# Moving part of a fused attention and mixer kernel's transposes from TensorE to the DMA crossbar

## The chip, the cores and the metric

The kernel runs on one core of a Trainium2 chip. The metric is device microseconds (us) of one execution, the median of several runs. Before the change it is 288.36 us (three runs, 288.26 to 288.44). Beside the times there is one profiled execution, whose span from the first to the last instruction is 287.1 us.

## The reference

Block-sparse attention over 4 batches with 8 heads, 768 positions and 64 elements for each head, and then a token mixer and a channel mixer on its result:

```python
# attention: q, k, v are [4, 8, 768, 64]; the mask is made of 32x32 blocks
scores = scale * np.matmul(q, k.transpose(0, 1, 3, 2))
mask = np.abs(blk_i - blk_j) <= window          # window = 1, and the edge blocks,
...                                             # and 3 sampled blocks for each row of blocks
scores = np.where(mask, scores, -1000000000.0)
attn = np.exp(scores - max) / sum
x = (attn @ v), heads side by side               # [4, 768, 512]

# mixer
h = np.maximum(xt @ w_tok1, 0.0) @ w_tok2        # xt is x transposed: mixes the 768 tokens
u = x + h.transpose(0, 2, 1)
h2 = np.maximum(u @ w_ch1, 0.0) @ w_ch2          # mixes the 512 channels, 1536 in the middle
return u + h2                                    # float32
```

## The kernel before

Two heads form a pair; there are 16 pairs, four in each batch. The work is put in order by a small planner inside the kernel's Python code: it keeps an expected time for each engine, holds streams of TensorE work by priority (scores first, then attention times V, then transposes, then the token mixer, then the channel mixer), and emits whatever is ready first. The chip then executes each engine's instructions in exactly that order, and waits where an operand is not there.

One pair's Q and K come in by DMA, are put by VectorE into a layout with the two heads side by side, are transposed by TensorE in six blocks of 128x128, and are copied out of PSUM, one head at a time, into `ktb` and `qtb`. Rows 64 to 87 of these hold the block mask, so that the scores' matmul over 88 rows adds it:

```python
def transposes(p):
    ...
    lays = relayout(p)                          # VectorE: kraw -> klay, qraw -> qlay, vraw -> vaug
    for nm, bufs, there in (("k", ktb, kT_there), ("q", qtb, qT_there)):
        for c in range(NC):                     # NC = 6
            nc.tensor.matmul(out=box["t"][:, c, :], lhsT=lays[nm][:, c, :, :]...,
                             rhs=ident[:, :], ..., is_transpose=True)
            deps = [lays[nm + "ev"]]
            if p >= NV:                         # NV = 4 sets of ktb and qtb
                deps.append(qk_done[p - NV])
        for hd in range(2):                     # copies out of PSUM, by VectorE or ScalarE
            nc.vector.tensor_copy(out=buf[0:64, :], in_=i)          # L439
...
# scores, exponentials (L470, L478): 12 steps for each pair, 192 in all
nc.tensor.matmul(out=ps[:, hd, 0:384], lhsT=ktb[n][0:88, 128*j : 128*j+128],
                 rhs=qtb[n][0:88, 384*half : 384*half+384])         # twice in a step
nc.scalar.activation(out=et[:, :, :], in_=ps[:, :, 0:384], func=AF.Exp, scale=0.125)
# attention times V (L520): 6 small matmuls in a step
nc.tensor.matmul(out=po[:, hd, c, :], lhsT=et[:, hd, 128*c : 128*c+128], rhs=va[:, hd, j, 0:65])
```

The token mixer of a batch (L578, L603) leaves `u`, in two halves `g` of 256 channels. `u` is transposed by TensorE (L628), six blocks for each of four groups of 128 channels, and copied out of PSUM (L641), since the channel mixer needs the channels on the partitions:

```python
for dmc in (2 * g, 2 * g + 1):
    for sc in range(NC):
        nc.tensor.matmul(out=tbox["pt"][:, sc, :], lhsT=st[b]["u"][:, sc, 128*dmc : 128*dmc+128],
                         rhs=ident[:, :], ..., is_transpose=True)   # L628
    evac ...                                                        # L641
# channel mixer: 96 matmuls of 384 columns (L664) and 72 of 512 (L686) for each batch
nc.tensor.matmul(out=pbox["pm"][:, 0:384], lhsT=w_ch1[:, dmc, 128*cc : 128*cc+128],
                 rhs=st[b]["uT"][:, dmc, 384*sh : 384*sh+384], ...)
nc.tensor.matmul(out=pbox["pm"][:, :], lhsT=box["rc"][:, cc, 128*sc : 128*sc+128],
                 rhs=w_ch2[:, cc, :], ...)
```

Transposes and both mixers share three PSUM buffers (`psM`, tag `pm`). While an exponential is pending, the planner gives ScalarE nothing else.

Of the kernel before, what the change touches and what calls it, by code (L numbers as in the profile page):

```python
# [50 lines left out]
class Planner:  # L51
# [11 lines left out]
    def __init__(self, slots):  # L63
        self.now = 0.0
        self.free_at = {"pe": 0.0, "act": 0.0, "dve": 0.0}
        self.streams = []
        self.ops = []
        self.count = 0
        self.slots = {tag: [Ev(0.0)] * n for tag, n in slots.items()}
        self.exp_pending = 0  # L70
# [6 lines left out]
    def op(self, engines, cost, deps, emit, prio=5, lat=60.0):  # L77
        done = Ev()
        self.ops.append((prio, self.count, engines, cost, deps, emit, done, lat))
        self.count += 1  # L80
        return done
# [21 lines left out]
    def step(self):  # L103

        nxt = []
        moved = False
        if self.free_at["pe"] <= self.now:
            for s in self.streams:
                while s[3] is None or (callable(s[3]) and s[3]()):
                    s[3] = next(s[2], False)  # L110
                if s[3] is False or callable(s[3]):
                    continue
                cost, deps, tags, emit, done = s[3]
                t = self.when(deps, tags)
                if t is None:
                    continue
                if t <= self.now:
                    s[3] = None
                    emit()
                    if self.trace is not None:  # L120
                        self.trace.append((self.now, "pe", s[0], cost))
                    self.free_at["pe"] = self.now + cost
                    if done is not None:
                        done.t = self.now + cost + self.PE_LAT + self.SEM
                    moved = True
                    break
                nxt.append(t)
            self.streams = [s for s in self.streams if s[3] is not False]
        else:
            nxt.append(self.free_at["pe"])  # L130
        for eng in ("act", "dve"):
            if self.free_at[eng] > self.now:
                nxt.append(self.free_at[eng])
                continue
            best = None
            for o in self.ops:
                prio, num, engines, cost, deps, emit, done, lat = o
                if eng not in engines:
                    continue
                if eng == "act" and prio > 0 and self.exp_pending:  # L140
                    continue
                t = self.when(deps)
                if t is None:
                    continue
                if t <= self.now:
                    if best is None or (prio, num) < best[:2]:
                        best = o
                else:
                    nxt.append(t)
            if best is not None:  # L150
                prio, num, engines, cost, deps, emit, done, lat = best
                self.ops.remove(best)
                emit(eng)
                c = cost[eng]
                if self.trace is not None:
                    self.trace.append((self.now, eng, prio, c))
                self.free_at[eng] = self.now + c
                done.t = self.now + c + lat + self.SEM
                moved = True
        if moved:  # L160
            return True
        later = [t for t in nxt if t > self.now]
        if not later:
            return False
        self.now = min(later)
        return True
# [3 lines left out]
def kernel(  # L170
# [22 lines left out]
    NET = 8  # L193

# [14 lines left out]
    qtb = [sb1.tile([128, S], BF16, name=f"qtb{n}") for n in range(2 * NV)]  # L209
    ktb = [sb1.tile([128, S], BF16, name=f"ktb{n}") for n in range(2 * NV)]  # L210

    P = Planner({"ps": 2, "po": 1, "pm": 3, "et": NET, "a_t": 2, "o": 3, "rc": 2,
                 "lay": 2, "kq": NV, "va": NV})
# [112 lines left out]
    rows_there = {("k", n): Ev() for n in range(2 * NV)} | {("q", n): Ev() for n in range(2 * NV)}  # L326

    def mask_stream():
# [15 lines left out]
        for h in range(2):  # L344
            def copy(eng, h=h):
                nc.scalar.copy(out=qtb[0][R, 384 * h : 384 * h + 384], in_=pms[h][R, 0:384])
            e2.append(P.op(("act",), {"act": 420.0}, [done], copy, prio=0))
            rels[h].same_as = e2[h]
        rows_there["q", 0].same_as = e2[1]
        for n in range(2 * NV):  # L350
            for nm, bufs in (("k", ktb), ("q", qtb)):
                if (nm, n) == ("q", 0):
                    continue

                def copy(eng, n=n, nm=nm, bufs=bufs):
                    nc.vector.tensor_copy(
                        out=bufs[n][R, :], in_=indf if nm == "k" else qtb[0][R, :]
                    )
                rows_there[nm, n].same_as = P.op(
                    ("dve",), {"dve": 300.0}, e2, copy, prio=2 if n < 2 else 6  # L360
                )
# [5 lines left out]
    ones_there = [Ev() for _ in range(NV)]  # L367

# [14 lines left out]
    def relayout(p):  # L383
        lays = {}
        for nm in ("k", "q", "v"):
# [3 lines left out]
            def emit(eng, nm=nm, raw=raw):  # L389
                if nm == "v":  # L390
                    nc.vector.tensor_copy(out=vaug[p % NV][:, :, :, 0:64], in_=raw[:, :, :, :])  # L391
                    return
                lay = sbw.tile([128, NC, 2, D], BF16, tag=f"{nm}lay", bufs=2, name=f"{nm}lay{p}")
                nc.vector.tensor_copy(  # L394
                    out=lay[:, :, :, :], in_=raw[:, :, :, :].rearrange("p h c d -> p c h d")
                )
                lays[nm] = lay
# [4 lines left out]
            if nm != "v" and p >= 2:  # L402
                deps.append(qT_there[p - 2, 1])
# [4 lines left out]

    def transposes(p):
        for hd in range(2):  # L410
            kT_there[p, hd], qT_there[p, hd] = Ev(), Ev()
        yield lambda: ("v", p) in raws
        lays = relayout(p)
        for nm, bufs, there in (("k", ktb, kT_there), ("q", qtb, qT_there)):
# [15 lines left out]
            n_left = [2]  # L430
            for hd in range(2):
                buf = bufs[2 * (p % NV) + hd]

                def evac(eng, hd=hd, buf=buf, box=box):
                    i = box["t"][64 * hd : 64 * hd + 64, :, :].rearrange("p c s -> p (c s)")
                    if eng == "act":
                        nc.scalar.copy(out=buf[0:64, :], in_=i)
                    else:
                        nc.vector.tensor_copy(out=buf[0:64, :], in_=i)  # L439
# [17 lines left out]
    def qk_stream():  # L457
        for s in steps:
# [4 lines left out]
            def emit(s=s, done=done, rel=rel):  # L463
# [4 lines left out]
                for hd in range(2):  # L468
                    n = 2 * (p % NV) + hd
                    nc.tensor.matmul(  # L470
                        out=ps[:, hd, 0:384], lhsT=ktb[n][0:88, 128 * j : 128 * j + 128],
                        rhs=qtb[n][0:88, 384 * half : 384 * half + 384], start=True, stop=True,
# [3 lines left out]
                def exp(eng):  # L476
# [13 lines left out]
                [e for hd in range(2) for e in (  # L490
                    kT_there[p, hd], qT_there[p, hd],
                    rows_there["k", 2 * (p % NV) + hd], rows_there["q", 2 * (p % NV) + hd],
# [8 lines left out]
    def pv_stream():  # L501
        for s in steps:
# [3 lines left out]
            def emit(s=s, done=done):  # L506
# [23 lines left out]
                def norm(eng):  # L530
                    if b not in xs:
                        xs[b] = sbw.tile([128, NC, DM], BF16, tag="x", bufs=B, name=f"x{b}")
# [3 lines left out]
                        out=free(xs[b][:, 3 * half, 128 * pb : 128 * pb + 128], 0,  # L536
                                 [[64, 2], [DM, 3], [1, 64]]),
# [29 lines left out]

    def tok(b, g):
# [3 lines left out]
        for t in range(2):  # L572
            for sc in range(NC):
                def emit(t=t, sc=sc):
                    if t == 0 and sc == 0:
# [4 lines left out]
                        rhs=xs[b][:, sc, 256 * g : 256 * g + 256],  # L580
# [4 lines left out]
        if b not in st:  # L585
            st[b] = dict(u=xs[b], uT_there=[Ev() for _ in range(4)])
# [6 lines left out]
        for s2 in range(3):  # L593
# [16 lines left out]
            def add(eng, s2=s2, ubox=ubox):  # L610
                nc.vector.tensor_tensor(  # L611
                    out=st[b]["u"][:, 2 * s2 : 2 * s2 + 2, 256 * g : 256 * g + 256],
                    in0=ubox["pm"][:, :, :],
                    in1=xs[b][:, 2 * s2 : 2 * s2 + 2, 256 * g : 256 * g + 256], op=ALU.add,
# [5 lines left out]
        alias(a_rel, last)  # L620
        for dmc in (2 * g, 2 * g + 1):
            last, rel, tbox = Ev(), Ev(), {}
            for sc in range(NC):
                def emit(sc=sc, dmc=dmc, rel=rel, tbox=tbox):
                    if sc == 0:
                        P.take("pm", rel)
                        tbox["pt"] = psM.tile([128, NC, 128], BF16, tag="pm", name=f"pm_ut_{b}_{dmc}")
                    nc.tensor.matmul(  # L628
                        out=tbox["pt"][:, sc, :], lhsT=st[b]["u"][:, sc, 128 * dmc : 128 * dmc + 128],
                        rhs=ident[:, :], start=(sc == 0), stop=(sc == NC - 1), is_transpose=True,  # L630
                    )
                yield 56.0, [u_evs[sc // 2]], [("pm", 1)] if sc == 0 else [], emit, last if sc == NC - 1 else None

            def evac(eng, dmc=dmc, tbox=tbox):
                if "uT" not in st[b]:
                    st[b]["uT"] = sbw.tile([128, 4, S], BF16, tag="uT", bufs=B, name=f"uT{b}")
                o, i = st[b]["uT"][:, dmc, :], tbox["pt"][:, :, :].rearrange("p c s -> p (c s)")
# [9 lines left out]
    def ch(b, pool, tag):  # L647
# [4 lines left out]
        for cc in range(12):  # L652
            for sh in range(2):
                last, rel, pbox = Ev(), Ev(), {}
                for dmc in range(4):
                    first = dmc == 0
                    def emit(cc=cc, sh=sh, dmc=dmc, rel=rel, pbox=pbox):
                        if dmc == 0:
# [7 lines left out]
                            rhs=st[b]["uT"][:, dmc, 384 * sh : 384 * sh + 384],  # L666
# [11 lines left out]
                rc_there[cc, sh] = ev  # L678
        for sc in range(NC):
# [12 lines left out]
            def fin(eng, sc=sc, pbox=pbox):  # L692
                o = sbw.tile([128, DM], FP32, tag="o", bufs=3, name=f"o{b}_{sc}")
                nc.vector.tensor_tensor(  # L694
                    out=o[:, :], in0=pbox["pm"][:, :], in1=st[b]["u"][:, sc, :], op=ALU.add
# [37 lines left out]
    P.stream(-1, mask_stream())  # L733
    tok2_op = P.op(("dve",), {"dve": 900.0}, [tok2_raw], wtok2_lay, prio=3)
# [57 lines left out]
```

The softmax here doesn't subtract the row's maximum and nothing guards it: scores larger than these inputs give would overflow.

## Time and profile before

| | before |
|---|---|
| time, median of 3 | 288.36 us |
| span of the profiled execution | 287.1 us |
| ScalarE, exponentials (L478) | 192 instructions, 143.2 us busy |
| TensorE, transposes of K and Q (L421) | 96 + 96 instructions |
| TensorE, transposes of u (L628) | 96 instructions |
| VectorE, copies of transposed K and Q (L439) | 59 instructions, 552 ns each (5 more on ScalarE) |
| VectorE, copies of transposed u (L641) | 15 instructions, 553 ns each (1 more on ScalarE) |
| TensorE, channel mixer, first product (L664) | 384 instructions |
| last load of K, Q or V issued | 91.5 us |

In the profile each engine has a row of busy time and of instructions. PE is TensorE's matmuls and PEld its weight loads, DVE is VectorE, ACT is ScalarE, POOL is GpSimd and SP is SyncE. Matmuls overlap in the pipeline and a matmul's listed duration is from its start to its modelled end, so the time that one matmul costs TensorE is read from the distance between the starts of neighbours, and not from its duration.

### The profile page before, as it was taken

Reading aid. Unit: us, or ns where it says so; the run is one execution under the profiler, and the core shown is the slowest. Engines: PE = TensorE matmul, PEld = TensorE weight load, DVE = VectorE, ACT = ScalarE, POOL = GpSimd, SP = SyncE. Lnnn points to the kernel's source line nnn. Section 1 sums busy time; section 2 is a strip of 40 time slices with the busy share of each in tenths; the row PEclk is TensorE's granted clock in tenths of the full one; section 3 lists DMA queues with packets and bytes.
Section 4 is the critical chain, followed back from the end, with each engine's and each line's share of the span. In section 5 each row is a group of like instructions: output and inputs, shape, how many; then the busy total and the mean of one; then the engine's idle time right before and its main releaser. Section 6 shows DMA issues by size and latency. Waiting matters only on the chain.

```text
span 287.1 us, 6351 instructions
## 1 busy us (share of the span) xinstructions
PE 269.9 (94%) x2682; PEld 175.5 (61%) x2690; DVE 130.2 (45%) x286; ACT 191.9 (67%) x286; POOL 45.0 (16%) x70
## 2 busy tenths in 40 slices
PE   0799899999999999999999999999999999999994
PEld 0366676678777777777777754456544654456441
DVE  5789966557777569765546341210022001200121
ACT  1589999999999999999999642037501770067200
POOL 7956554522211000000000000000000000000000
PEclk9999999999999999999999999999999999999999
DMA  4999999996254100000000001220022001210122
GB/s 55 134 204 202 214 201 205 201 185 87 39 73 66 23 2 2 0 2 3 2 0 2 2 0 39 106 76 0 2 110 84 29 0 73 94 54 0 38 102 82
DMA packets 19168, 20.07 MB, mean 70 GB/s; under 512 B 1348, under 2 KB 15428, under 8 KB 19140
## 3 DMA queue, kind: packets, MB, share of 16 engines
q0 software_dynamic: 15648, 13.37, 30.3%
q1 hardware_dynamic: 3492, 6.29, 5.8%
q8 instruction: 21, 0.34, 0.5%
q14 instruction: 7, 0.06, 0.1%
HBM read 26.74 MB, written 6.29 MB: 115 GB/s over the span
## 4 chain that ended last, share of the span: by engine, by line
PE 73%; ACT 14%; DVE 6%; issue 2%; DMA 2%; POOL 2%; POOLq 0%; DVEq 0%; ACTq 0%
PE pm_ch L686 22%; PE pm_ch L664 21%; ACT et L478 14%; PE ps L470 14%; PE po L520 8%; PE pm_tok L578 3%; PE pm_tok L603 2%; DMA kraw<-in_k_dram 2%; DVE qtb L439 1%; PE pm_ut L628 1%; PE tq L421 1%; DVE ktb L439 1%; PE tk L421 1%; DVE x L535 1%; DVE klay L394 1%
## 5 line engine op out<-in xcount | busy, mean ns | idle before, releaser
L478 ACT ACTIVATE et<-ps 128x768 bf16<-128x768 f32 x192 | 143.2, 810 | 4.2 <-PE ps L470 3.2
L470 PE MATMUL ps<-qtb,ktb 88*128 88x384 bf16 x384 | 95.3, 329 | 4.0 <-ACT et L478 1.7
L560 ACT ACTIVATE rc<-pm_ch 128x384 bf16<-128x384 f32 x84 | 41.2, 491 | 60.7 <-PE pm_ch L664 44.8
L520 PEld LDWEIGHTS <-et 128*128 128x128 bf16 x1152 | 56.0, 97 | 22.8 <-DVE x L535 1.9
L664 PE MATMUL pm_ch<-uT,w_ch 128*128 128x384 bf16 x384 | 68.6, 326 | 0.2 <-DVE rc L562 0.2
L686 PE MATMUL pm_ch<-w_ch,rc 128*128 128x512 bf16 x280 | 62.4, 379 | 0.4
L520 PE MATMUL po<-vaug,et 128*128 128x65 bf16 x1152 | 61.5, 193 | 0.5 <-ACT et L478 0.2
L694 DVE TENSOR_TENSOR o<-pm_ch,x 128x512 f32<-128x512 f32 x24 | 16.6, 692 | 98.7 <-PE pm_ch L686 98.7
L664 PEld LDWEIGHTS <-w_ch 128*128 128x128 bf16 x384 | 37.0, 98 | 23.1 <-issue 0.3
L686 PEld LDWEIGHTS <-rc 128*128 128x128 bf16 x288 | 28.2, 98 | 33.6
L470 PEld LDWEIGHTS <-ktb 88*128 88x128 bf16 x384 | 34.2, 99 | 11.9 <-issue 4.4
L439 DVE COPY ktb<-tk 64x768 bf16<-64x768 bf16 x29 | 16.0, 552 | 17.5 <-PE tk L421 17.2
L611 DVE TENSOR_TENSOR x<-pm_tok,x 128x512 bf16<-128x512 f32 x24 | 16.2, 687 | 6.8 <-PE pm_tok L603 6.5
L535 DVE TENSOR_TENSOR x<-po,recip 128x384 bf16<-128x384 f32 x32 | 17.8, 557 | 1.1
L439 DVE COPY qtb<-tq 64x768 bf16<-64x768 bf16 x30 | 16.6, 552 | 2.1 <-PE tq L421 1.1
L603 PE MATMUL pm_tok<-a_t,w_tok 128*128 128x256 bf16 x96 | 17.0, 272 | 0.0
L230 POOL DMA_DIRECT2D vraw<-in_v_dram x16 | 12.3, 766 | 28.4 <-DVE vaug L391 25.7
L578 PE MATMUL pm_tok<-x,w_tok 128*128 128x256 bf16 x96 | 16.3, 272 | 0.0
L230 POOL DMA_DIRECT2D kraw<-in_k_dram x16 | 11.6, 727 | 7.7 <-DVE recip L534 2.2
L230 POOL DMA_DIRECT2D qraw<-in_q_dram x16 | 11.5, 720 | 6.4 <-DMA w_ch<-in_moe_w_ch_dram 2.4
L534 DVE RECIPROCAL recip<-po 128x6 f32<-128x6 f32 x32 | 6.2, 195 | 12.0 <-PE po L520 11.6
L421 PE MATMUL tq<-ident,qlay 128*128 128x128 bf16 x96 | 11.3, 230 | 0.2 <-DVE qlay L394 0.2
(49 smaller groups left out, 122.8 us busy)
## 6 DMA issues: line engine op xcount, KB each, us to landing
out_dram<-o SPq DMA_DIRECT2D x24, 256.0 KB, 2.0
kraw<-in_k_dram POOLq DMA_DIRECT2D x16, 192.0 KB, 7.9
qraw<-in_q_dram POOLq DMA_DIRECT2D x16, 192.0 KB, 7.4
vraw<-in_v_dram POOLq DMA_DIRECT2D x16, 192.0 KB, 7.0
w_ch<-in_moe_w_ch_dram POOLq DMA_DIRECT2D x8, 384.0 KB, 9.8
w_tok<-in_moe_w_tok_dram POOLq DMA_DIRECT2D x1, 384.0 KB, 7.8
w_tok2r<-in_moe_w_tok_dram POOLq DMA_DIRECT2D x1, 384.0 KB, 9.0
samp<-in_sampled_blocks_dram SPq DMA_DIRECT2D x1, 0.6 KB
```

The lines of the kernel that those rows point to most:

```text
L230: nc.gpsimd.dma_start(out=raw[:, :, :, :], in_=APx(src, 2 * p * S * D, [[NC * D, 128], [S * D, 2], [1, NC * D]]),)
L421: nc.tensor.matmul(out=box["t"][:, c, :], lhsT=lays[nm][:, c, :, :].rearrange("p h d -> p (h d)"), rhs=ident[:, :], start=(c == 0), stop=( ...
L439: nc.vector.tensor_copy(out=buf[0:64, :], in_=i)
L470: nc.tensor.matmul(out=ps[:, hd, 0:384], lhsT=ktb[n][0:88, 128 * j : 128 * j + 128], rhs=qtb[n][0:88, 384 * half : 384 * half + 384], star ...
L478: nc.scalar.activation(out=et[:, :, :], in_=ps[:, :, 0:384], func=AF.Exp, scale=0.125)
L520: nc.tensor.matmul(out=po[:, hd, c, :], lhsT=et[:, hd, 128 * c : 128 * c + 128], rhs=va[:, hd, j, 0:65], start=(j == 0 and hd == 0 and c = ...
L535: nc.vector.tensor_tensor(out=free(xs[b][:, 3 * half, 128 * pb : 128 * pb + 128], 0, [[64, 2], [DM, 3], [1, 64]]), in0=po[:, :, :, 0:64], ...
L560: nc.scalar.activation(out=o(), in_=i, func=AF.Relu)
L578: nc.tensor.matmul(out=box["pm"][:, t, :], lhsT=w_tok1[:, sc, 128 * t : 128 * t + 128], rhs=xs[b][:, sc, 256 * g : 256 * g + 256], start=( ...
L603: nc.tensor.matmul(out=ubox["pm"][:, i, :], lhsT=w_tok2[:, t, 2 * s2 + i, :], rhs=a_t[:, t, :], start=(i == 0 and t == 0), stop=(i == 1 an ...
L664: nc.tensor.matmul(out=pbox["pm"][:, 0:384], lhsT=w_ch1[:, dmc, 128 * cc : 128 * cc + 128], rhs=st[b]["uT"][:, dmc, 384 * sh : 384 * sh + ...
L686: nc.tensor.matmul(out=pbox["pm"][:, :], lhsT=box["rc"][:, cc, 128 * sc : 128 * sc + 128], rhs=w_ch2[:, cc, :], start=(cc == 0), stop=(cc ...
```

## The change

Twelve of the 32 transposes of a K or Q pair (those of pairs 10 to 15) and the transposes of u of batches 1 to 3 are done by the DMA queue of SyncE, with a transposing transfer from SBUF to SBUF through the crossbar. The rest stays on TensorE. The change is for relieving TensorE, VectorE and PSUM of the transposes and their copies. It leaves the early pairs alone, whose transposes fall into the time in which K, Q, V and the weights are being loaded.

For pairs 10 to 15 the layout copy writes a wider tile, `kwide` or `qwide`, with 128 columns for each head: 64 of data, 24 of the mask, 40 of zeros. The mask and the zeros are written once. One transfer then turns all 12 blocks of 128x128, and its result, mask rows included, goes straight into `ktb` or `qtb`. There are two such wide tiles for each of K and Q. For u one transfer turns one half `g` of a batch, which is 12 blocks too. To make its source contiguous, `x` (and `u`, which overwrites it) is laid out as `[128, 2, NC, 256]`.

```diff
+    NPE = 10
+    NL = 2
...
-    qtb = [sb1.tile([128, S], BF16, name=f"qtb{n}") for n in range(2 * NV)]
+    qtb = [sb1.tile([128, 2, S], BF16, name=f"qtb{n}") for n in range(NV)]      # ktb too
+    wide = {
+        (nm, n): sb1.tile([128, 2, NC, 128], BF16, name=f"{nm}wide{n}")
+        for n in range(NL) for nm in ("k", "q")
+    }
...
+    def wide_stream():                       # once, from 60 us of the plan on
+            box["m"] = psM.tile([128, 2, NC, 24], FP32, tag="pm", name="pm_wide")
+            for i, rhs in enumerate((ident[R, 64:88], t2add[R, :])):
+                for c in range(NC):
+                    nc.tensor.matmul(out=box["m"][:, i, c, :], lhsT=ind[R, c, :], rhs=rhs, ...)
+        ... for each of the four wide tiles:
+                    nc.vector.memset(wide[nm, n][:, :, :, 64:128], 0.0)
+                    nc.vector.tensor_copy(out=wide[nm, n][:, :, :, 64:88], in_=...)
...
-                lay = sbw.tile([128, NC, 2, D], BF16, tag=f"{nm}lay", bufs=2, name=f"{nm}lay{p}")
+                elif p >= NPE:
+                    nc.vector.tensor_copy(out=wide[nm, p % NL][:, :, :, 0:64], in_=raw[:, :, :, :])
+                else:
+                    lay = sbw.tile([128, NC, 2, D], BF16, tag=f"{nm}lay", bufs=1, name=f"{nm}lay{p}")
...
-            if nm != "v" and p >= 2:
-                deps.append(qT_there[p - 2, 1])
+            if nm != "v" and 1 <= p < NPE:
+                deps.append(qT_there[p - 1, 1])
+            if nm != "v" and p >= NPE:
+                deps.append(wide_there[nm, p % NL])
+                if p - NL >= NPE:
+                    deps.append(xb_done[nm, p - NL])
...
+    def crossbar(p):
+                nc.sync.dma_start_transpose(
+                    out=bufs[p % NV][:, :, :].rearrange("e h (c s) -> e (h c) s", c=NC),
+                    in_=wide[nm, p % NL][:, :, :, :].rearrange("p h c e -> p (h c e)"),
+                )
+            deps = [lays[nm + "ev"]]
+            if p >= NV:
+                deps.append(qk_done[p - NV])
+            ev = P.op(("sp",), {"sp": 1600.0}, deps, emit, prio=1, lat=5000.0)
...
+    def turn_by_crossbar(b, g, u_evs):
+            nc.sync.dma_start_transpose(
+                out=st[b]["uT"][:, g, :, :, :].rearrange("e c m p -> e (c m) p"),
+                in_=st[b]["u"][:, g, :, :].rearrange("p c e -> p (c e)"),
+            )
+        ev = P.op(("sp",), {"sp": 1600.0}, u_evs, emit, prio=2, lat=4000.0, ...)
...
+        if b > 0:
+            turn_by_crossbar(b, g, u_evs)
+            return
...
-                            rhs=st[b]["uT"][:, dmc, 384 * sh : 384 * sh + 384],
+                            rhs=st[b]["uT"][:, dmc // 2, 3 * sh : 3 * sh + 3, dmc % 2, :],
```

What is left out above: the planner's new row `sp` for SyncE's queue, and the adapted index expressions of the other users of `x`, `u`, `ktb` and `qtb`. `uT` has three buffers instead of four, and `klay` and `qlay` have one instead of two, which makes room for the wide tiles.

## The prediction

> **What bounds the kernel now.** I read the busy time by stretches first, since the page's averages mix two stages. The columns are the stretch, its length, and then busy us and instructions of PE, PEld, DVE, ACT and POOL.
>
> ```profile
> 60.00:100.00 40.00, 39.95 (x564) 30.46 (x563) 28.13 (x64) 39.73 (x54) 7.16 (x10) 1.00 0.51 72
> 100.00:160.00 60.00, 59.75 (x846) 45.87 (x845) 37.64 (x81) 59.70 (x81) 0.00 (x0) 1.00 0.01 2
> 168.00:287.10 119.10, 114.55 (x604) 59.75 (x611) 17.07 (x26) 40.13 (x82) 0.00 (x0) 1.00 0.14 54
> ```
>
> Up to 160 us ScalarE is full: it does almost nothing but exponentials, 138 by the ACT column of the windows of 20 us from 60 to 160, so 0.725 us each. From 168 us on ScalarE is idle two thirds of the time and TensorE has all the work. The chain of waits, in order of time, tells what that work is (start, length, engine and line):
>
> ```profile
> 189.61 15.60 PE pm_ch L664 x96
> 205.48 10.74 PE pm_ch L686 x49
> 216.27 4.48 PE pm_ch L686 x20
> 220.75 15.60 PE pm_ch L664 x96
> 236.62 10.74 PE pm_ch L686 x49
> 247.41 4.48 PE pm_ch L686 x20
> 251.89 15.60 PE pm_ch L664 x96
> ```
>
> Three whole channel mixers, 31.14 us each (220.75 - 189.61), stand after the attention, back to back. One matmul of L664 costs 15.60 / 96 = 0.1625 us. The tail can't wait for anything; it gets shorter only if TensorE does part of the channel mixer before 160 us.
>
> Is TensorE really full before 160 us? The busy share says so, but it also says 19.08 of 20 us from 40 to 60 us, where I find holes. Here are two steps from about 46 us in the timeline of TensorE, with L470 the scores and L520 attention times V:
>
> ```profile
> 46.34 0.48 PE L470 MATMUL ps<-qtb,ktb 88*128 88x384 bf16 x2
> 46.66 0.35 PE L520 MATMUL po<-vaug,et 128*128 128x65 bf16 x6
> 47.05 0.48 PE L470 MATMUL ps<-qtb,ktb 88*128 88x384 bf16 x2
> 47.37 0.34 PE L520 MATMUL po<-vaug,et 128*128 128x65 bf16 x6
> 47.78 0.48 PE L470 MATMUL ps<-qtb,ktb 88*128 88x384 bf16 x2
> ```
>
> From start to start, the scores cost 0.33 us. The six L520 matmuls cost 0.18 us where another follows at once, as in the next fence (107.48 - 107.30). A step takes 0.72 us, so 0.2 us of it is free and, here, unused: the channel mixer has not got its inputs yet. So I count TensorE by starts and not by busy time. And here is a place that is full, at 107 us:
>
> ```profile
> 106.57 0.34 PE L520 MATMUL po<-vaug,et 128*128 128x65 bf16 x6
> 106.75 0.39 PE L421 MATMUL tk<-ident,klay 128*128 128x128 bf16 x4
> 106.97 0.49 PE L470 MATMUL ps<-qtb,ktb 88*128 88x384 bf16 x2
> 107.30 0.34 PE L520 MATMUL po<-vaug,et 128*128 128x65 bf16 x6
> 107.48 0.27 PE L421 MATMUL tk<-ident,klay 128*128 128x128 bf16 x2
> ```
>
> The transposes sit in the gap between L520 and the next L470. Four take 106.97 - 106.75 = 0.22 us, so **one transpose costs 0.055 us**, a quarter of its listed 0.23 us.
>
> The count for 60 to 160 us: 138 steps of 0.505 us are 69.7; 133 token mixer matmuls at 0.109 (two take 106.24 - 106.02 = 0.22 us in the same timeline) are 14.5; 96 transposes of K and Q and 72 of u at 0.055 are 9.2; 39 L664 matmuls at 0.1625 are 6.3. Sum 99.7 of 100 us. So after 60 us TensorE and ScalarE are both full, ScalarE sets the pace, and TensorE's filler decides how much of the channel mixer is left for the tail. Only about 60 of the 384 L664 matmuls are done by 168 us (384 less 36 and 3 x 96 in the chain after it).
>
> **What the Trainium skill says.** "VectorE: DVE Perf Modes", section "The three transpose paths", gives 390 ns for a 128x128 transpose on TensorE and 1309 ns through the DMA crossbar. For a stream of them on TensorE this trace disagrees: 55 ns. "Perfetto Trace Analysis", section "Identifying the Most-Contended Engine", says that matmul busy time is not a good measure; the trace agrees, as the 46 us fence showed. "DMA: Bandwidth & Descriptors", section "Latency and other measured facts", gives 261 GB/s for a DMA transpose that isn't contiguous; no run here shows one yet. The same page, "Rules for kernel authors", says that transposes from different queues must be serialized and that one beside ordinary DMAs needs nothing. Here all are issued from SyncE, so nothing should have to be put in between.
>
> **The change part by part.**
>
> 1. *Removed from TensorE:* 6 pairs x 12 = 72 transposes of K and Q, and 3 batches x 24 = 72 of u. 144 x 0.055 = **7.9 us**. Of these, 12 (u of the last half batch, 0.7 us) stood after 160 us, the others before it.
> 2. *Added to TensorE:* 12 matmuls of 24 columns for the mask, once. With the 0.03 us that a 65-column matmul costs in the stream (0.18 / 6), 0.4 us.
> 3. *Where the gain appears.* Before 160 us it isn't time that is saved, since ScalarE keeps the pace there. It is room: 7.2 - 0.4 = 6.8 us, or some 42 L664 matmuls more. With the 39 of before that makes 81 before 160 us, within the 96 of batch 0, whose inputs are there from about 65 us. So all the room can be used and the tail gets shorter by it, and by the 0.7 us after 160 us. Sum: 7.5 us.
> 4. *What filling with larger pieces costs.* A transpose fits into a 0.2 us gap anywhere; an L664 matmul of 0.16 us only once, and then delays the next scores or leaves 0.06 us open. I choose 0.5 us off for it, a judgement and not a count.
> 5. *VectorE:* 24 copies of K and Q at 0.552 us and 12 of u at 0.553 us fall away: 19.9 us, nearly all VectorE's. In return, 42 L664 matmuls need some 10 copies of 0.551 us before 160 us (5.8), and the wide tiles 4 clears and 4 copies: with the 698 ns of the 24x768 memset and the plan's 0.45 us for a copy, 4.6 us in all. VectorE is busy 66 of 100 us here, so it isn't a limit before or after.
> 6. *The crossbar.* 12 transfers for K and Q and 6 for u, each 128 x 1536 x 2 bytes = 0.39 MB. At the skill's 261 GB/s one is an estimated 1.5 us of transfer; the planner assumes 1.6 us and 5 us until it lands. The only measured row for SyncE's queue is the output's (transfer, count, KB, us to landing):
>
> ```profile
> out_dram<-o SPq DMA_DIRECT2D x24, 256.0 KB, 2.0
> ```
>
> So 3 to 6 us until landing is my estimate. The need: pair p's transfers may start once the scores of pair p-4 are done, and are read when pair p starts, three pairs or 3 x 12 x 0.725 = 26 us later. So two transfers in turn have 26 us. The queue as a whole has 18 transfers between about 76 us (84 exponentials done) and 166 us, 5 us for each. Below 4.7 us a piece, taken in turn, nothing waits.
> 7. *One layout buffer instead of two* makes a pair's layout copy wait for the last pair's transposes. In the first 35 us, where VectorE has a queue of copies, the layout copies already come after the last pair's copies out of PSUM, except once at 30.7 us. I count nothing for it, with up to 0.5 us either way.
>
> So 288.4 - 7.5 + 0.5 = 281.4. Around 166 us TensorE's listed idle times (0.19, 0.31 and 0.20 us) are waits for the last u's additions and for PSUM buffers that its transposes hold; about half of these 0.7 us should go, which brings me to **281.0 us**.
>
> **The rivals.**
>
> *The crossbar is slow and becomes the pace.* At 8 us a transfer in turn, 18 would be 144 us in a stretch of 90. Then the scores of pairs 11 to 15 wait, ScalarE stands idle, and the time goes to 295 or more. For it: no run has shown such a transfer's time, and 1309 ns for one block would be 15.7 us for twelve if they went one after another. Against it: the 261 GB/s and the planner's 1.6 us, whose other constants (0.326 for a step's scores, 0.1625 for L664) are just what the trace shows.
>
> *The plan is too hopeful in latency.* A pair's layout copy into a wide tile waits for the transfer of the pair two before. VectorE runs in order. If the transfer lands 3 us later than planned, VectorE stands that long, with the normalization of the attention result behind it, and the single `po` buffer stops TensorE. There are eight such copies (4 pairs, K and Q), so 2 to 6 us could be given back: 283 to 287. For it: only two wide tiles. Against it: eight buffers of exponentials hold some 6 us.
>
> *The room isn't used.* If the three PSUM buffers or the copies limit the channel mixer before 160 us, the tail stays and only 1 to 3 us come. For it: the mask's matmuls hold one of the three buffers until the last wide tile is written. Against it: transposes held the same buffers, 36 fewer copies are to be made, and the count above shows that all the room was in use.
>
> *The transfers collide with loads.* The last V load is issued at 91.5 us and the DMA share is 0.51 between 60 and 100 us, so pairs 10 and 11 still meet loads. They have the 26 us, so I expect nothing of it in the time.
>
> **Range and chances.** If all goes by the count: 280 to 282, to which I give some 65%. Partial losses by late transfers or unused room: 282 to 287, 25%. Over 287: 10%. Upwards there is little: 7.9 us plus the 0.7 us of waits gives 279.8, and a luckier start perhaps 279. A gain of 2% needs 5.8 us, that is, less than 1.7 us lost of the 7.5.
>
> **What will show it.** Step 1: 60 transposes each of K and Q are left, and 24 of u, and 36 fewer copies out of PSUM. Step 3: exponentials still at 0.725 us each to about 160 us, and some 80 or more L664 matmuls before 160 us; the three whole mixers at the end still 31.14 us each and the last starting some 7 us sooner. Step 6: transfers landing within 6 us, and no waits of TensorE's scores or VectorE's layout copies on them. The prediction is wrong if the waits name the transposing transfers, if ScalarE's idle time before 160 us grows by more than 1 us, or if TensorE's starts show holes of 0.2 us after 70 us where mixer work should stand.

## The result and the profile after

| | before | after |
|---|---|---|
| time, median of 4 | 288.37 us | 277.18 us (277.15 to 277.31) |
| ratio to before | | 0.9613 (95% interval 0.9596 to 0.963) |
| span of the profiled execution | 287.1 us | 275.6 us |

The change saves 11.2 us, 3.9%. The prediction was 281.0 us with a range from 279.0 us; the measured time lies below the range.

First the busy time by stretches, cut where the stages of the changed kernel end. The columns are the stretch, its length, then busy us and instructions of PE, PEld, DVE, ACT and POOL, the granted clock, the DMA share and GB/s.

```profile
60.00:100.00 40.00, 39.55 (x545) 29.44 (x543) 27.32 (x65) 39.86 (x54) 7.17 (x10) 1.00 0.92 140
100.00:157.00 57.00, 57.00 (x746) 41.76 (x744) 27.71 (x62) 56.78 (x77) 0.00 (x0) 1.00 0.42 63
```

ScalarE is as full as before up to the end of the attention. From 100 us VectorE is busy 27.71 of 57 us, where it had 37.64 of 60. The DMA share between 60 and 100 us is now 0.92, before 0.51. The chain of waits has the same tail (start, length, engine and line; L753 and L776 are the channel mixer's two products; shown are the second of the three whole mixers and the first half of the third):

```profile
209.29 15.60 PE pm_ch L753 x96
224.89 15.54 PE pm_ch L776 x72
240.43 15.60 PE pm_ch L753 x96
```

Each of the three whole mixers still takes 31.14 us (240.43 - 209.29), but the last begins at 240.43 and not at 251.89 us: 11.46 us sooner. And the transfers, from the list of DMA issues (transfer, queue, count, median us from issue to landing):

```profile
ktb<-kwide SPq DMA_TRANSPOSE x6, 4.6
qtb<-qwide SPq DMA_TRANSPOSE x6, 5.3
uT<-x SPq DMA_TRANSPOSE x6, 4.0
```

They land after 3.7 to 5.8 us, within the 3 to 6 us of the estimate. In the whole list of waits, one line names one of them, and it is short (engine, line, what it waited for: us in total, times, longest):

```profile
DVE qwide L432 <- DMA qtb<-qwide: 0.6, 1, 0.6
```

So the transposes are hidden, as predicted. Where do 3.8 us more than predicted come from? The cost of every TensorE instruction, by starts and not by busy time (0.1625 us for a matmul of 384 columns, 0.216 for 512, 0.109 for 256, 0.030 for 65, 0.055 for a transpose), is summed for each stretch and taken from its length. What is left is TensorE without work:

| us from the start | before | after |
|---|---|---|
| 20 to 40 | 3.8 | 3.1 |
| 40 to 60 | 2.4 | 0.7 |
| 60 to 80 | 0.4 | 1.7 |
| 80 to 155 | 2.1 | 0.3 |
| 155 to 170 | 0.8 | none |

That is 9.5 us before and some 5.8 us after: 3.7 us of holes less, beside the 7.5 us of work less. The largest piece, 2.4 us, lies between 20 and 60 us, where the change puts nothing on the crossbar. In the timeline of the kernel before, TensorE's scores (L470) leave a hole after 31 us, and 11 matmuls of the token mixer (L578) come ahead of the next ones:

```profile
30.65 0.48 PE L470 MATMUL ps<-qtb,ktb 88*128 88x384 bf16 x2
33.00 1.51 PE L578 MATMUL pm_tok<-x,w_tok 128*128 128x256 bf16 x11
34.34 0.88 PE L470 MATMUL ps<-qtb,ktb 88*128 88x384 bf16 x4
```

The next scores are the first of pair 2. Its Q and K had long been turned. What was missing is its second head's mask row, copied into `qtb` by VectorE at L356:

```profile
34.17 0.35 DVE L356 COPY qtb<-qtb 24x768 bf16<-24x768 bf16 x1
```

The first head's matmul starts at 34.34 us, and the second head's at 34.57 us, just after this copy has ended at 34.52 us. Little of the hole is waiting on the chip: the planned order itself has other work ahead of these scores. These copies have the plan's lowest priority, and VectorE was busy running ahead with K and Q of pairs 3, 4 and 5. In the changed kernel (scores at L533) the hole is gone:

```profile
30.53 0.49 PE L533 MATMUL ps<-qtb,ktb 88*128 88x384 bf16 x2
31.25 0.48 PE L533 MATMUL ps<-qtb,ktb 88*128 88x384 bf16 x2
31.98 0.48 PE L533 MATMUL ps<-qtb,ktb 88*128 88x384 bf16 x2
32.69 0.48 PE L533 MATMUL ps<-qtb,ktb 88*128 88x384 bf16 x2
```

The only part of the change that can act on this so early is the layout gate: one `klay` and `qlay` instead of two, which keeps the layout copies from running ahead. What the hole delays is ScalarE, which sets the pace of the attention. Here are its last exponentials before (L478) and after (L542):

```profile
139.68 21.23 ACT L478 ACTIVATE et<-ps 128x768 bf16<-128x768 f32 x28
139.34 18.90 ACT L542 ACTIVATE et<-ps 128x768 bf16<-128x768 f32 x25
```

They end at 160.91 us before and at 158.24 us after, 2.67 us sooner.

### The profile page after: what moved, and what is told of

Read it like the earlier page. It is cut to its first block, busy times and chain, and to the rows that moved or that the text cites. A ratio compares the mean times of both kernels' runs of the same rounds, so it can differ in the third digit from the quotient of the medians.

```text
span 275.6 us, 6123 instructions
## 1 busy us (share of the span) xinstructions
PE 261.2 (95%) x2558; PEld 167.8 (61%) x2558; DVE 121.9 (44%) x272; ACT 184.3 (67%) x272; POOL 44.6 (16%) x70
## 3 DMA queue, kind: packets, MB, share of 16 engines
q1 hardware_dynamic: 31716, 13.37, 22.3%
## 4 chain that ended last, share of the span: by engine, by line
PE 79%; ACT 11%; DVE 6%; issue 1%; POOL 1%; POOLq 0%; ACTq 0%
PE pm_ch L776 23%; PE pm_ch L753 23%; PE ps L533 17%; ACT et L542 11%; PE po L583 9%; PE pm_tok L686 3%; PE pm_tok L661 3%; DVE qtb L502 1%; DVE ktb L502 1%; PE tk L487 1%; PE tq L487 1%; DVE klay L435 0%; DVE w_tok L797 0%; DVE x L598 0%; PE pm_ut L715 0%
## 5 line engine op out<-in xcount | busy, mean ns | idle before, releaser
L542 ACT ACTIVATE et<-ps 128x768 bf16<-128x768 f32 x192 | 143.7, 809 | 3.7 <-PE ps L533 2.9
L533 PE MATMUL ps<-qtb,ktb 88*128 88x384 bf16 x384 | 95.9, 331 | 3.0 <-ACT qtb L500 1.6
L625 ACT ACTIVATE rc<-pm_ch 128x384 bf16<-128x384 f32 x74 | 36.3, 491 | 60.1 <-PE pm_ch L753 44.1
L753 PE MATMUL pm_ch<-uT,w_ch 128*128 128x384 bf16 x384 | 71.7, 326 | 0.0
L583 PEld LDWEIGHTS <-et 128*128 128x128 bf16 x1152 | 56.3, 97 | 22.5 <-issue 1.4
L776 PE MATMUL pm_ch<-w_ch,rc 128*128 128x512 bf16 x288 | 63.1, 379 | 0.0
L583 PE MATMUL po<-vaug,et 128*128 128x65 bf16 x1152 | 61.5, 193 | 0.0
L753 PEld LDWEIGHTS <-w_ch 128*128 128x128 bf16 x384 | 36.2, 98 | 21.1
L776 PEld LDWEIGHTS <-rc 128*128 128x128 bf16 x288 | 28.2, 98 | 33.1
L533 PEld LDWEIGHTS <-ktb 88*128 88x128 bf16 x384 | 35.1, 99 | 12.3 <-issue 2.7
L627 DVE TENSOR_SCALAR rc<-pm_ch 128x384 bf16<-128x384 f32 x22 | 12.2, 553 | 13.9 <-PE pm_ch L753 13.8
L502 DVE COPY ktb<-tk 64x768 bf16<-64x768 bf16 x19 | 10.5, 551 | 4.5 <-PE tk L487 4.3
L502 DVE COPY qtb<-tq 64x768 bf16<-64x768 bf16 x19 | 10.5, 554 | 1.8 <-PE tq L487 1.0
```

The lines of the kernel that those rows point to most:

```text
L502: nc.vector.tensor_copy(out=buf[0:64, hd, :], in_=i)
L533: nc.tensor.matmul(out=ps[:, hd, 0:384], lhsT=ktb[n][0:88, hd, 128 * j : 128 * j + 128], rhs=qtb[n][0:88, hd, 384 * half : 384 * half + 38 ...
L583: nc.tensor.matmul(out=po[:, hd, c, :], lhsT=et[:, hd, 128 * c : 128 * c + 128], rhs=va[:, hd, j, 0:65], start=(j == 0 and hd == 0 and c = ...
L625: nc.scalar.activation(out=o(), in_=i, func=AF.Relu)
```

## The experiments

Theory A: the gate removes the hole at the start, worth 2.6 us, and the rest is TensorE's time for 144 transposes. Theory B: all comes from the transposes and their copies out of PSUM, which cost more than TensorE's time for them. Ratios are to the kernel before. Times are medians of four runs, and the ratios leave out the slow runs, which took over 1.5% longer than the fastest of the same kernel: one in each of four experiments (the gate alone, whose profiled run took 984.11 us; `NPE = 8`; the same with the 12 us; the changed kernel with the wide tiles sooner), and three with each transfer twice to the same place.

### The start

**The gate alone**, on the kernel before:

```diff
-                lay = sbw.tile([128, NC, 2, D], BF16, tag=f"{nm}lay", bufs=2, ...)
+                lay = sbw.tile([128, NC, 2, D], BF16, tag=f"{nm}lay", bufs=1, ...)
-            if nm != "v" and p >= 2:
-                deps.append(qT_there[p - 2, 1])
+            if nm != "v" and p >= 1:
+                deps.append(qT_there[p - 1, 1])
```

> The kernel before with the change's layout gate alone (one klay and one qlay, a pair's layout copy only after the last pair's transposes are copied out); no crossbar. Theory A (the start: the gate keeps VectorE from running ahead to pairs 4 and 5, so the mask rows of pair 2 are written sooner and the scores don't stand from 31 to 34 us): 2.6 us less than before, about 285.7 us. Theory B (all 11.2 us come from the transposes and copies taken away): as before, 288.4 us.

Measured: 286.33 us, ratio 0.9918 (0.9901 to 0.9934), that is, 2.4 us less.

**The mask rows sooner**, on the kernel before, with the gate as it was:

```diff
-                    ("dve",), {"dve": 300.0}, e2, copy, prio=2 if n < 2 else 6
+                    ("dve",), {"dve": 300.0}, e2, copy, prio=2 if n < 6 else 6
```

> The kernel before with one edit: the mask rows of pairs 1 and 2 get the priority of the first pair's. Theory A: the same cure by another way, about 285.7 us, and no hole in the scores between 31 and 34 us. Theory B: as before, 288.4 us. If the gate helps and this does not, the mask rows were not the cause.

Measured: 286.28 us, ratio 0.993 (0.9905 to 0.9954), 2.0 us less. The hole is gone from the scores in its timeline of TensorE:

```profile
31.29 0.48 PE L470 MATMUL ps<-qtb,ktb 88*128 88x384 bf16 x2
32.03 0.48 PE L470 MATMUL ps<-qtb,ktb 88*128 88x384 bf16 x2
32.73 0.48 PE L470 MATMUL ps<-qtb,ktb 88*128 88x384 bf16 x2
```

**The change without the gate**: the first edit the other way round, on the changed kernel.

> The changed kernel with the old layout gate and two layout buffers for the early pairs; all crossbar transposes stay. Theory A: the hole of the start comes back, 277.2 + 2.6 = 279.8 us. Theory B: as the changed kernel, 277.2 us.

Measured: 280.02 us, ratio 0.9705 (0.9689 to 0.9721), 2.65 us slower than the changed kernel's 0.9613 (0.0092 x 288.4). This is inside the predicted range.

**The change without the gate, with the mask rows sooner**: both edits on the changed kernel.

> The changed kernel with the old layout gate and two layout buffers, and with the mask rows of pairs 1 and 2 at high priority. If the gate's gain is only that pair 2's mask rows come sooner: as the changed kernel, 277.2 us within 0.6 us. If the gate does something else besides: nearer to the 280.0 us of the run without the gate.

Measured: 277.95 us, ratio 0.9637 (0.9621 to 0.9653). Of the 2.65 us that the gate is worth, the order of the mask rows alone brings 2.0. The other 0.7 us is hardly beyond the intervals, and was not separated.

Theory A holds for the start: two edits that share nothing but the earlier mask rows each bring 2.0 to 2.65 us, with the crossbar or without it. The hole is gone in the traces of the changed kernel (gate) and of the run above (rows); the run of the gate alone shows it only by its time. The end of the exponentials says the same: 158.00 us with the rows sooner on the kernel before, 160.74 us in the change without the gate, 158.72 us in that with the rows sooner.

### The transposes

**K and Q alone on the crossbar**, on the changed kernel: u's transposes go back to TensorE for all batches, and their copies to VectorE and ScalarE.

```diff
-        if b > 0:
+        if b > B:
             turn_by_crossbar(b, g, u_evs)
```

> The changed kernel with all of u's transposes back on TensorE; K and Q of pairs 10 to 15 stay on the crossbar. If only TensorE's time for the transposes counts (72 x 0.055 us): 277.2 + 4.0 = 281.2 us. If copies and PSUM buffers count too (theory B): more, 282.5 us or over.

Measured: 282.05 us, ratio 0.9797 (0.9751 to 0.9843). Taking u off TensorE is worth 5.3 us by this, with an interval of over 1 us to either side (one of the four runs took 284.33 us; by the medians it is 4.9 us).

**u alone on the crossbar**: `NPE = 16`, no wide tiles, and four `uT` buffers.

> The changed kernel with K and Q of all pairs on TensorE and no wide tiles; u of batches 1 to 3 stays on the crossbar. Count of TensorE's time (72 x 0.055 us back, 0.4 us of mask matmuls gone): 277.2 + 3.6 = 280.8 us. If u's share is as large as the last runs make it (5.3 us of the whole against 3.3 us for K and Q): 280.5 us or less; if copies and PSUM make K and Q costlier than their time on TensorE: 282 us or more.

Measured: 281.34 us, ratio 0.9756 (0.9742 to 0.9771): K and Q are worth 4.1 us.

**TensorE's time for K and Q put back, and nothing else:** after the transfers, the kernel also does the 12 transposes of each pair from 10 on, into a PSUM tile that nobody reads. It needs four `uT` buffers.

```diff
             crossbar(p)
+            for nm in ("k", "q"):
+                for c in range(NC):
+                    nc.tensor.matmul(out=box["t"][:, c, :], lhsT=wide[nm, p % NL][:, 0, c, :],
+                                     rhs=ident[:, :], ..., is_transpose=True)
```

> The changed kernel with 12 transposes for each of pairs 10 to 15 put back on TensorE that nobody copies or reads; the crossbar still brings K and Q. Same output. If TensorE's time alone counts: 277.2 + 72 x 0.055 = 281.2 us. If what counted was the copies out of PSUM and the waits around them: under 279 us.

Measured: 281.19 us, ratio 0.9749 (0.9732 to 0.9765), 3.9 us over the changed kernel. The count was 72 x 0.055 = 4.0 us. The run with the copies out of PSUM as well (u alone on the crossbar) is no slower, although it also saves the making of the wide tiles, 0.4 us of TensorE's time by the prediction's count: the 24 copies cost nothing that these intervals show.

**The same for u:** 72 transposes of u in their old places, and nobody reads them; four `uT` buffers again.

> The changed kernel with u's 72 transposes put back on TensorE in their old places, but nobody copies or reads them; the crossbar still brings u. If TensorE's time alone counts: 277.2 + 4.0 = 281.2 us. If the whole 5.3 us sits in it, as in the run with u on TensorE: 282.5 us, that is, the waits of the transposes on u's additions, in TensorE's order, cost the rest. Under 280.5 us: the copies out of PSUM were a part of the cost.

Measured: 281.74 us, ratio 0.9769 (0.9754 to 0.9783), 4.5 us over the changed kernel, where 4.0 were counted. Most of u's 5.3 us is TensorE's own time and what it waits for in its order; whether the remaining 0.8 us is copies or noise stays open, within the interval of the run with u on TensorE (the two medians are 0.3 us apart). In these four runs the exponentials end between 158.08 and 158.43 us, as in the changed kernel: the transposes don't touch the pace of the attention, only what TensorE gets done beside it.

Theory B falls as an account of the whole. From the gate alone to the whole change, 0.0305 x 288.4 = 8.8 us go away, and from the kernel before to the change without the gate 0.0295 x 288.4 = 8.5 us, where the prediction had 7.5 less 0.5, and some 0.4 for waits at the end: 7.4.

### How much room the crossbar has

**Each transfer twice, to the same place**, on the changed kernel:

```diff
-                nc.sync.dma_start_transpose(...)
+                for _ in range(2):
+                    nc.sync.dma_start_transpose(...)
```

> The changed kernel with each of the 12 transfers of K and Q issued twice in a row, to the same place. The theory that the transfers are hidden (26 us from the earliest start to their use, 4 to 6 us each): 277.2 us, within 1 us. The rival that the queue or the wide buffers are near the pace: 3 us or more slower, with VectorE's layout copies or the scores waiting for the transfers.

Measured: 302.84 us, from 297.58 to 303.58. My expectation was wrong, and the experiment mixed two things: a second transfer into the same tile waits until the first has landed, and SyncE's queue stands behind it. The timeline of its queue shows pairs of transfers in 5.5 to 8 us:

```profile
76.57 7.96 SPq L462 DMA_TRANSPOSE ktb<-kwide  x2
84.58 5.55 SPq L462 DMA_TRANSPOSE qtb<-qwide  x2
90.22 6.21 SPq L462 DMA_TRANSPOSE ktb<-kwide  x2
96.47 7.77 SPq L462 DMA_TRANSPOSE qtb<-qwide  x2
```

With the transfer of u that follows at 104.29 us not yet counted, that is 27.7 us for two pairs of heads, where the attention needs 18 (24 steps of 0.75 us, as between 80 and 155 us of the changed kernel).

**Twice without that wait:** the second transfer goes into a spare tile, and the plan allows 3.2 us for the two.

> Each of the 12 transfers of K and Q is followed by a second one of the same size into a tile that nobody reads, and the plan allows 3.2 us of the queue for the two. No transfer waits for another. If the queue has room for 30 transfers between 76 and 162 us: 277.2 us within 1 us. If the 302.8 us of the run with two transfers to the same place were a matter of the queue's rate and not of the waits between the two: far over 280 us again.

Measured: 285.03 us, ratio 0.9882 (0.9839 to 0.9924), 7.8 us slower than the change. 24 transfers start between 75.26 and 129.97 us, one every 2.4 us. By an estimate from this rate, four for a pair take 9.6 us, and 12 with one for u, against 9 us of attention. A wide tile stays occupied until its second transfer has landed, and VectorE waits for it; from the waits between 74 and 160 us:

```profile
DVE qwide L433 <- DMA qspare<-qwide: 11.9, 3, 5.7
DVE kwide L433 <- DMA kspare<-kwide: 4.6, 4, 2.2
```

So the rival of a too slow crossbar is real, but the change as it stands is on the right side of it: with two transfers for a pair and one for u every second pair or so, 5 to 7 us out of 9. How much of the 7.8 us is the queue's rate was not separated: the plan still expected a wide tile to be free after 5 us, and a plan that is too early costs time by itself, as the next run shows.

**A plan that hopes for too much:** one number of the changed kernel's plan, the landing time of K's and Q's transfers.

```diff
-            ev = P.op(("sp",), {"sp": 1600.0}, deps, emit, prio=1, lat=5000.0)
+            ev = P.op(("sp",), {"sp": 1600.0}, deps, emit, prio=1, lat=1500.0)
```

> The changed kernel with the plan's landing time of K's and Q's transfers set to 1.5 us (measured: 4.6 and 5.3). The rival of the prediction that a too hopeful plan gives time back: VectorE's layout copies wait up to 3.5 us each, 279 us or more. If the exponential buffers and the distance of 26 us take it up: 277.2 us within 1 us.

Measured: 280.5 us, ratio 0.9726 (0.9706 to 0.9746), 3.3 us slower. VectorE's layout copies now stand in its order before the transfers have landed:

```profile
DVE kwide L432 <- DMA ktb<-kwide: 6.8, 4, 2.3
DVE qwide L432 <- DMA qtb<-qwide: 6.2, 3, 3.6
```

Only the planned order changed. The eight exponential buffers don't take such waits up.

### Beside the loads

**Pairs 8 and 9 on the crossbar too:** `NPE = 8`.

> The changed kernel with pairs 8 and 9 on the crossbar too, while loads still run. Hidden transfers: 24 x 0.055 = 1.3 us less, 275.9 us. The rival that transfers beside loads cost more than they give: 277.2 us or more, with later landings of K, Q and V.

Measured: 283.45 us, ratio 0.9826 (0.981 to 0.9843). It is 6.1 us slower than the changed kernel, with 24 transposes fewer on TensorE. The timeline of SyncE's queue shows what a transfer meets while the loads run, and the waits show who pays:

```profile
77.13 7.56 SPq L461 DMA_TRANSPOSE qtb<-qwide  x1
84.78 4.07 SPq L461 DMA_TRANSPOSE ktb<-kwide  x1
```

```profile
DVE kwide L432 <- DMA ktb<-kwide: 7.8, 3, 6.5
```

SyncE itself is held for up to 7.56 us in issuing one transfer, where it takes 1.44 us (K) and 1.83 us (Q) at the median in the changed kernel. The landings of K go up to 13.9 us.

VectorE's longest wait, 6.5 us, reaches TensorE, whose clock is lower after it. TensorE's timeline around it (L533 scores, L583 attention times V, L753 channel mixer; in brackets the idle time before and what ended it):

```profile
82.00 0.49 PE L533 MATMUL ps<-qtb,ktb 88*128 88x384 bf16 x2
82.33 0.34 PE L583 MATMUL po<-vaug,et 128*128 128x65 bf16 x6
87.97 0.48 PE L753 MATMUL pm_ch<-uT,w_ch 128*128 128x384 bf16 x1 [5.13 <-DVE x L694]
88.24 0.84 PE L533 MATMUL ps<-qtb,ktb 88*128 88x384 bf16 x2
88.88 0.54 PE L583 MATMUL po<-vaug,et 128*128 128x65 bf16 x6
```

After the hole a step's scores cost 0.64 us from start to start, where they cost 0.33 before it, and the granted clock is 0.50 from 88 to 92 us. So a part of the 6.1 us, not separated, is a slower TensorE after the wait. The same stands in the other runs with long holes: the clock is 0.83 on average between 60 and 80 us in the next run, 0.80 to 0.83 between 80 and 140 us with each transfer twice to the same place, and 0.91 between 120 and 140 us with the spare tile. In the run with the short landing time it stays at 1.00.

**The same with the wide tiles made ready 18 us sooner**, so that they don't hold back the loads:

> Pairs 8 and 9 on the crossbar too, and the wide tiles made ready 18 us sooner, so that the loads of pairs 12 and 13 are not held back by them. If the 283.4 us came from the held-back loads that then met the transfers: 276 to 278 us. If transfers beside any loads land late (over 8 us where 5 are planned) and VectorE, in order, waits for them: 280 us or more, with waits of the layout copies on the transfers.

Measured: 283.48 us, ratio 0.9821 (0.9802 to 0.984). No better: loads held back by the wide tiles were not the cause.

**And with an honest landing time in the plan**, 12 us for pairs 8 to 10:

```diff
+            ... prio=1, lat=12000.0 if p < 11 else 5000.0)
```

> The same with one number of the plan changed: the transfers of pairs 8 to 10 are planned to land after 12 us, not 5. If the loss is VectorE's in-order wait for a landing that the plan had too early: the waits go and it comes to about 275.9 us (24 x 0.055 us under the changed kernel). If the transfers themselves are too slow beside loads: no better than the run without it.

Measured: 281.04 us, ratio 0.9731 (0.9706 to 0.9755). The plan's number is worth 2.6 us, but 3.4 us against the changed kernel are left. The transfers now land after up to 15.7 us, so that 12 us was still too early, and VectorE has one long wait left:

```profile
DVE qwide L432 <- DMA qtb<-qwide: 3.6, 2, 3.4
```

TensorE's holes between 60 and 80 us come to 3.75 us, in which the lower clock from 78 us on is included (0.50 between 80 and 84 us). So both are true: the plan was too early, and the transfers beside loads are themselves too slow for it. A still longer landing time was not tried. That is why the change leaves the early pairs alone.

### An attempt to do better

The changed kernel has more holes than before between 60 and 80 us, 1.7 us. I made its wide tiles at 42 to 46 us of the plan instead:

> The changed kernel with the wide tiles made ready at 42 to 46 us of the plan instead of 60 to 64. If the hole of 1.7 us between 60 and 80 us comes from them (a PSUM buffer held, VectorE busy): about 276.2 us. If TensorE simply has no ready work there, because batch 0's u is not finished: 277.2 us.

Measured: 278.78 us, ratio 0.9656 (0.963 to 0.9683), no gain (1.2 us slower by the ratios). The hole shrinks to 1.3 us only, and VectorE waits 2.6 us for a transfer later, a side effect of the new order. No run here beats the changed kernel.

## Why the prediction was wrong

**The step that failed is the seventh**, the layout buffers, for which it counted nothing, "with up to 0.5 us either way". It measured 2.4 us on the kernel before and 2.65 us within the change, all to the good. The prediction had looked at the order of VectorE's copies, and had even named the one exception "at 30.7 us". It asked whether the layout copies themselves come later, and not what they keep waiting: the mask rows with the lowest priority, and behind them pair 2's scores. The hole was there to be read in the profile before, 3.7 us between two starts of L470. So "a luckier start", which the prediction left as a small chance, was not luck but an edit of the change itself. Without this term the change is the run without the gate, 280.02 us, 1 us from the predicted 281.0.

**Step 4 had the wrong sign.** The 0.5 us taken off for larger filler pieces did not show. Between 80 and 155 us TensorE's holes went from 2.1 to 0.3 us, and 77 L753 matmuls stand there instead of 26.

**The count behind step 3 had missed those holes.** It has 138 exponentials between 60 and 160 us, summed over five windows, and a window also counts what only reaches into it. One window over the whole stretch has 134, so 0.746 us each and not 0.725; it has 132 matmuls of the token mixer and 37 of L664. With the prediction's own costs that makes 134 x 0.505 + 132 x 0.109 + 168 x 0.055 + 37 x 0.1625 = 97.3 us, and not 99.7: TensorE was not full, 2.7 us were free. That the change gained a further 1 us or so by filling such holes fits this, but no run isolates it.

**Steps 1 and 3 held in their mechanism.** 0.055 us for a transpose gave 4.0 us for K and Q, and 3.9 us was measured by putting them back; for u 4.0 and 4.5. The exponentials kept their pace (101 between 80 and 155 us before, 100 after), and the tail's mixers their 31.14 us. The room before the end of the attention went into the channel mixer, as said: 95 L753 matmuls by 160 us, where the prediction had 81 and the kernel before 39.

**Step 6 held in its result and was off in its rate.** Nothing waits but 0.6 us. But the DMA page of the changed kernel puts q1, the queue of SyncE, at 22.3% of 16 engines' span, and before it was 5.8%. That is 61.5 - 16.7 = 44.8 us for 18 transfers, so 2.5 us for each, or 0.39 MB / 2.5 us = 158 GB/s. The estimate of 1.5 us, from the 261 GB/s of "DMA: Bandwidth & Descriptors" in the Trainium skill ("Latency and other measured facts"), was too short: 2.5 us is two thirds more. The measurement decides. The 2.4 us between starts in the run with a spare tile says the same.

**The rivals.** The room was used, so that one is out. The three on late transfers (a slow crossbar, a hopeful plan, collisions with loads) were judged rightly for this kernel, but it stands close to each of them: each became true as soon as one number moved, the number of transfers (7.8 us), the plan's landing time (3.3 us) or the first pair (6.1 us).

## What to carry to other kernels

A change that moves work to an idle engine can also reorder a stage that it does not touch: look in the profile before the change for holes in the stream that sets the pace (distances between starts, not busy shares) and ask of each edit whether it moves what ends them. In a kernel whose order is planned ahead, a latency in the plan that is too short costs time on an engine that runs in order, here 3.3 us for 3.5 us of optimism. And a transposing transfer is hidden only as long as its queue keeps the pace of the stage that it feeds, so count it in us for each step and not only in total.

## What the runs showed of the hardware

A crossbar transfer of 128 x 1536 two-byte elements from SBUF to SBUF cost 2.5 us of all 16 DMA engines, in some 1570 packets of about 250 bytes (q1 went from 3492 to 31716 packets). Beside loads, issuing it held SyncE for up to 7.56 us and it landed after up to 13.9 us. Putting K's and Q's transposes back on TensorE without their copies out of PSUM cost as much as with them (281.19 and 281.34 us), so in this kernel these copies, on a VectorE that is busy 44% of the changed kernel's span, cost nothing that could be measured; for u the difference, 0.8 us, is within the noise. After a hole of 5.1 us TensorE's granted clock was 0.50 from 88 to 92 us, and the scores of a step took 0.64 instead of 0.33 us.
